# Attention backward on one core: the four dV quarters of a block, one in each even unit and ahead of the output transposes

## The chip, the cores and the metric

The kernel runs on one core of one Trainium2 chip, in one launch. The metric is the device time of that core in microseconds (us); less is better. PE is TensorE (matmuls and transposes), ACT is ScalarE, DVE is VectorE, POOL is GpSimd, SP is the engine whose queue issues most DMAs.

## What is computed

The reference takes two attention layers over the same kind of input (2048 tokens, width 448, 16 heads of 28) and returns their joined output together with the gradients of all eight inputs. Layer A is a linear attention; layer B is a softmax attention in which all 16 heads share one key and one value head. The change is in the backward pass of layer B:

```python
scores = jnp.einsum("bhqd,bkd->bhqk", q, k) * (Dh ** -0.5)
p = _softmax(scores, axis=-1)
o = jnp.einsum("bhqk,bkd->bhqd", p, v)
_out, _vjp = jax.vjp(_f, A_x, A_wqkv, A_wo, B_x, B_wq, B_wk, B_wv, B_wo)
_grads = _vjp(grad_out)
```

For layer B the core loop needs, for every pair of heads and every group of queries, the exponentials E of the scores, the output O = E V / sum, the gradient dP = dO Vᵀ, the product dS = E * dP (the row term is folded into an added column), and from these dQ = dS K, dK = dSᵀ Q and dV = Eᵀ dO.

## The kernel before, in words

Layer A and the projections of layer B come first (the span's first 208 us). Then the core loop `for u in range(NU + 28)` (from L926) runs over 512 **units** and a tail. A **block** b is 8 units: two heads and 256 queries against all 2048 keys; a unit takes two tiles of 128 keys. There are 64 blocks. In this document "unit k" means any u with u % 8 = k. All instructions are issued in the order in which the code is written (`manual_schedule`), so each engine's queue has that order, and only semaphores make it wait.

The loop is a software pipeline, and one pass of it works on several blocks at once. In unit u:

- `rows_SD` (L683) puts eight **row matmuls** on PE (tiles of 32 rows by 128 columns, 256 elements each): four give the scores of unit u in two PSUM banks (`aacc`, two of the three in `SB`), four give dP of unit u - 16 in the two banks `DB` (`agen`). In odd units the order is score 0, score 1, dP 0, dP 1, and again; in even units the two matmuls of dP 1 come last.
- ACT takes three instructions: the exponential of score 0 (L946, "exp 0"), the copy of dP 1 to `cp` (L960), the exponential of score 1 (L992, "exp 1"). DVE multiplies dP 0 by E to the first half of `dsT` (L958), POOL does the second half out of `cp` (L961), and DVE transposes the `dsT` of unit u - 18 in 32 x 32 squares to `dsx` (L1039).
- In odd units `dk_m` puts 16 dK matmuls on PE (tiles of 32 x 32, 512 elements). In even units `o_dq` puts 16 matmuls for O and dQ of two units on PE (tiles of 128 rows by 32 columns, 256 elements).

Some work comes once in a block, through the third bank of `SB`, called `spare`. It is the bank that exp 1 of unit u - 1 reads and that score 0 of unit u + 1 is written to:

- unit 2: `onat_T` (L806) puts the block's end product O back into its natural layout with two fp32 transposes (PE, L809; tiles of 64 x 128). `o_norm` takes it from there: a reciprocal (DVE, L818) and a product (DVE, L819), both read from `spare`. POOL then makes `prod` and `don` (L823 to L827).
- unit 4: `row_D` (L831, L832) finishes `don`.
- unit 6: `don_T` (L834 to L840) transposes `don` into `spare` (128 x 32 tiles), `don_copy` (DVE, L847) takes it out.
- unit 0 of most blocks: a part of the output projection (`out_proj`, 128 x 32 tiles, 112 columns, or 224 in ten blocks) or, in early blocks, of dO's projection goes through `spare`, and DVE copies it out (L747 or L913).
- unit 1: DVE copies O from the accumulator (L974). Unit 3: DVE copies dQ (L977).

The **dV quarters** are `dv_mm(dv_acc, b, h, qb)` (L896): four matmuls side by side (128 x 32 tiles, 512 elements each) that add head h and query half qb of block b to a PSUM bank of their own. Their moving operand is `eN`, which a DMA transpose on SP's queue makes of four units of exponentials at a time (L994); `eN` has six buffers, two to a block. Their weights are `don`, which has three buffers. Before the change the quarters stand at the end of the PE work of a unit, behind `o_dq`: quarters 0 and 1 of block b in unit 8b + 20 (unit 4), quarter 2 in 8b + 22 (unit 6), quarter 3 in 8b + 26 (unit 2). Unit 0 has none.

Of the kernel before, what the change touches and what calls it, by code (L numbers as in the profile page):

```python
# [25 lines left out]
def kernel(  # L26
# [620 lines left out]
    NB = 64  # L647
# [3 lines left out]
    with ExitStack() as cs_:  # L651
# [20 lines left out]
        def eN(b, c):  # L672
            return ENs[(2 * b + c // 2) % 6][:, 16 * (c % 2):16 * (c % 2) + 16, :]

        def mmt(out, lhsT, rhs, pos, start, stop):
            nc.tensor.matmul(out, lhsT=lhsT, rhs=rhs, start=start, stop=stop, tile_position=pos,  # L676
                             skip_group_check=True)

        def blk(b):
            qc, pair = divmod(b, 8)  # L680
            return qc, pair, pair // 2, pair % 2

        def rows_SD(u, sp, dp):  # L683
            b, tp = divmod(u, 8)
            w = u - 16
            qc, pair, g, hp = blk(b)
            todo = [(0, 0), (0, 1), (1, 0), (1, 1)] * 2
            if sp is not None and dp is not None and u % 2 == 0:
                todo = [(0, 0), (0, 1), (1, 0)] * 2 + [(1, 1)] * 2
            seen = {}  # L690
            for d in todo:
                if (dp if d[0] else sp) is None:
                    continue
                k, h = d
                t2 = seen.get(d, 0)
                seen[d] = 1
                t = 2 * tp + t2
                tc_ = slice(t * P, (t + 1) * P)
                oc = slice(t2 * 256, (t2 + 1) * 256)
                r = 64 * (1 - hp if k else hp) + 32 * h  # L700
                if k:
                    mmt(dp[h][:, oc], vT_rep[r:r + 32, tc_], doT[w // 8][r:r + 32, :], (r, 0), True, True)
                else:
                    mmt(sp[h][:, oc], kT_rep[r:r + 32, tc_], qT_B[g][r:r + 32, qc * 256:(qc + 1) * 256],
                        (r, 0), True, True)
# [96 lines left out]
        def due(u, lag):  # L802
            b, r = divmod(u - lag, 8)
            return b if r == 0 and 0 <= b < NB else None

        def onat_T(b, bank):  # L806
            onp = bank[:, 0:P].rearrange("p (q h c) -> p q h c", q=2, h=2)
            for qb in range(2):
                nc.tensor.transpose(onp[:, qb, :, :].rearrange("p h c -> p (h c)"), oTs[0:64, qb * P:(qb + 1) * P],  # L809
                                    identF[0:64, 0:64], tile_position=(0, 0))  # L810
            onps[b] = onp
# [48 lines left out]
        def dk_m(b, m, other=0):  # L860
            qc, pair, g, hp = blk(b)
            h, B, s = m // 8, (m // 2) % 4, m % 2
            for a in range(4):
                rhs = dsx[b][32 * a:32 * a + 32, :, h, :, :].rearrange(
                    "p u t (b i s) -> p u t b i s", b=4, s=2)[:, :, :, B, :, s]
                k = 32 * ((a + 2) % 4) if other else 32 * a
                mmt((dk_two if other else dk_acc)[k:k + 32, :],
                    qX[qc][32 * a:32 * a + 32, B, s, pair * 64 + 32 * h:pair * 64 + 32 * h + 32],
                    rhs, (32 * a, k), other == 2 or b == 0 and m == 0, other == 0 and b == NB - 1 and m == 15)
# [19 lines left out]
        def o_dq(vs, ys):  # L889
            for v, y in zip(vs, ys):  # L890
                todo = [f(i) for f, i in ((o_mm, v), (dq_mm, y)) if 0 <= i < NU]
                for _ in range(2):
                    for g_ in todo:
                        next(g_)

        def dv_mm(dv_acc, b, h, qb):  # L896
            for c in range(4):
                rhs = eN(b, c).rearrange("p (u h t q) k -> p u h t q k", u=2, h=2,
                                                       t=2)[:, :, h, :, qb, :]
                mmt(dv_acc[32 * c:32 * c + 32, :], don[b][:, qb, h, :], rhs, (0, 32 * c),  # L900
                    b == 0 and h + qb == 0, b == NB - 1 and h + qb == 2)
# [15 lines left out]
        with tc.manual_schedule():  # L917
# [8 lines left out]
            for u in range(NU + 28):  # L926
# [4 lines left out]
                dp = DB if hasD else None  # L931
                spare = SB[(2 * u + 2) % 3] if hasS else DB[u // 4 % 2] if u > 530 else SB[2]
                rows_SD(u, sp, dp)
                if (b := due(u, 10)) is not None:
                    onat_T(b, spare)
                if (b := due(u, 14)) is not None:
# [10 lines left out]
                if u == 1:  # L947
                    q_shift(pn3, shifts[3], [pd_.tile([P, 2, 512], BF16, name="dsT").rearrange("p a b -> p (a b)").bitcast(F32)
                                             for _ in range(1)])
                    dv_acc = psA.tile([P, 512], F32, name="aacc")  # L950
# [48 lines left out]
                if u % 2:  # L999
                    b, i = divmod(u - 27, 8)  # L1000
                    if 0 <= b < NB:
                        for m in range(2 * i, 2 * i + 4):
                            dk_m(b, m, (1 + (u == 519 and m == 2 * i + 1)) * (m % 2) if 519 <= u < 537 else 0)
                else:
                    o_dq((u - 2, u - 1), (u - 20, u - 19))
                    b, n = divmod(u - 20, 8)
                    for k in {0: (0, 1), 2: (2,), 6: (3,)}.get(n, ()) if 0 <= b < NB else ():
                        dv_mm(dv_acc, b, k // 2, k % 2)
                y = u - 18

                if 512 <= u < 528 and u % 2 == 0:
# [23 lines left out]
                if 0 <= y < NU:  # L1035
                    b, tp = divmod(y, 8)
# [115 lines left out]
```

## Time and profile before

| what | value |
|---|---|
| median of 3 runs | 1052.08 us (1051.96 to 1053.91) |
| the profiled execution, its own time | 1052.68 us |
| its span in the trace | 1050.9 us (1.8 us lie outside it) |
| busy in the span: PE, DVE, ACT, POOL | 96%, 85%, 83%, 76% |
| core loop with scores (units 0 to 511) | 207.7 to 977.0 us |
| one block of 8 units, steady | 11.97 and 12.03 us, in turn |
| granted TensorE clock | 1.00 |

A block is found in the trace by ACT's exponentials, of which the loop has 512 pairs, one per unit. Two things help to read the tables. The matmuls' starts are recorded and their ends are modelled, and matmuls on different tiles run side by side, so PE's 96% is the time in which any matmul is open, not time at peak. And where DVE or ACT work back to back, an instruction starts some hundredths of a us before the one ahead of it has ended, so the step from start to start, and not the duration, says what an instruction costs there.

### The profile page before, as it was taken

To read this page: it belongs to the slowest core of one execution; us is meant where nothing else is said; L and a number is where in the kernel's file an instruction comes from. 1 tells how busy PE (TensorE), PEld (TensorE's weight loads), DVE (VectorE), ACT (ScalarE), POOL (GpSimd) and SP (SyncE) were. 2 spreads that over 40 slices of the span, in tenths; PEclk is the share of its full clock that TensorE was granted. 3 is DMA by queue.
4 is the path that set the end of the run, shared out by engine and by line. 5 is a ranking of instruction groups with operands and counts; after the bars stand their busy time and mean duration, and the time that the engine had idled before them with its cause. 6 is when DMAs were issued, how large, how long until landed. Compare 5 with 4: busy or idle time off the path is not lost.

```text
span 1050.9 us, 40033 instructions
## 1 busy us (share of the span) xinstructions
PE 1008.4 (96%) x16236; PEld 486.6 (46%) x16245; DVE 895.9 (85%) x1781; ACT 871.5 (83%) x1743; POOL 798.2 (76%) x1044
## 2 busy tenths in 40 slices
PE   9999999998999999999999999999999999999998
PEld 5555554434444444444444444444444444444444
DVE  6897500669999999999999999999999999999942
ACT  6463122589999999999999999999999999999632
POOL 8601272238888998899899989988998999888860
PEclk9999999999999999999999999999999999999999
DMA  9879999299999999999999999999999999999973
GB/s 266 150 134 192 189 222 215 42 163 202 188 196 190 188 195 198 194 193 191 197 175 195 192 202 185 204 199 184 192 194 191 194 190 193 204 186 182 220 156 87
DMA packets 689058, 195.15 MB, mean 186 GB/s; under 512 B 670408, under 2 KB 686688, under 8 KB 688872
## 3 DMA queue, kind: packets, MB, share of 16 engines
q1 hardware_dynamic: 680392, 179.97, 102.1%
q0 software_dynamic: 4544, 9.46, 3.4%
q10 hardware_dynamic: 3936, 3.16, 1.0%
q8 instruction: 127, 2.08, 0.8%
q14 instruction: 59, 0.48, 0.1%
HBM read 12.60 MB, written 10.84 MB: 22 GB/s over the span
## 4 chain that ended last, share of the span: by engine, by line
PE 44%; ACT 33%; issue 14%; DVE 6%; POOL 2%; DMA 0%; ACTq 0%; DVEq 0%; POOLq 0%
ACT cp L960 17%; ACT eT L992 13%; PE agen L81 13%; PE aacc L676 10%; PE agen L676 10%; PE aacc L81 6%; ACT eT L946 2%; DVE dsT L958 2%; PE aacc L809 2%; DVE dsx L1039 2%; PE aacc L840 1%; POOL dsT L961 1%; DMA out_dram<-dsT 0%; PE agen L313 0%; PE agen L227 0%
## 5 line engine op out<-in xcount | busy, mean ns | idle before, releaser
L961 POOL TENSOR_TENSOR dsT<-cp,eT 128x512 bf16<-128x512 bf16 x512 | 587.7, 1156 | 78.9 <-ACT cp L960 73.2
L1039 DVE STREAM_TRANSPOSE dsx<-dsT 128x512 f32<-128x512 f32 x512 | 357.8, 699 | 2.8 <-POOL dsT L961 0.7
L676 PEld LDWEIGHTS <-R 32*128 32x128 bf16 (+1 forms) x9104 | 228.5, 94 | 275.0 <-issue 239.4
L958 DVE TENSOR_TENSOR dsT<-agen,eT 128x512 bf16<-128x512 f32 x512 | 341.9, 668 | 10.6 <-PE agen L676 5.4
L960 ACT ACTIVATE cp<-agen 128x512 bf16<-128x512 f32 x512 | 315.8, 617 | 11.5 <-PE agen L676 10.5
L946 ACT ACTIVATE eT<-aacc 128x512 bf16<-128x512 f32 x512 | 313.6, 612 | 13.6 <-PE aacc L676 4.3
L992 ACT ACTIVATE eT<-aacc 128x512 bf16<-128x512 f32 x512 | 322.2, 629 | 0.0
L676 PE MATMUL agen<-dsx,qX 32*32 32x512 bf16 x4024 | 264.0, 376 | 0.0
L676 PE MATMUL agen<-doT,R 32*128 32x256 bf16 x2048 | 246.7, 269 | 4.2 <-DVE dsT L958 2.5
L676 PE MATMUL aacc<-R,R 32*128 32x256 bf16 (+1 forms) x2240 | 218.5, 269 | 7.1 <-DVE oTs L819 2.0
L676 PE MATMUL agen<-eT,R 128*32 128x256 bf16 x2048 | 157.4, 274 | 0.1
L676 PE MATMUL agen<-dsT,R 128*32 128x256 bf16 x2048 | 156.6, 274 | 0.1
L676 PEld LDWEIGHTS <-qX 32*32 32x32 bf16 x4096 | 78.2, 89 | 111.7 <-issue 53.3
L676 PE MATMUL aacc<-eN,don 128*32 128x512 bf16 x1024 | 96.7, 379 | 0.0
L81 PEld LDWEIGHTS <-R 128*128 128x128 bf16 x517 | 40.9, 98 | 42.2 <-issue 12.0
L81 PE MATMUL agen<-R,R 128*128 128x448 bf16 (+1 forms) x174 | 41.1, 360 | 1.8 <-ACT R L229 0.8
L851 POOL COPY qst<-R 128x512 bf16<-128x512 bf16 x56 | 34.2, 611 | 2.9 <-DMA qX<-qst 2.8
L823 POOL TENSOR_TENSOR prod<-R,oTs 128x128 f32<-128x128 bf16 x64 | 27.6, 431 | 9.3 <-DVE oTs L819 9.3
L676 PEld LDWEIGHTS <-don 128*32 128x32 bf16 x1024 | 33.8, 97 | 0.5
L586 DVE TENSOR_TENSOR osb<-R 32x512 bf16<-32x512 bf16 x4 | 1.7, 413 | 34.7 <-ACT R L583 34.7
L262 POOL TENSOR_SCALAR wdq<-wdq 128x448 bf16<-128x448 bf16 x16 | 21.1, 1327 | 12.9 <-DVE phiT L243 12.9
L427 POOL COPY pk<-R 128x256 bf16<-128x256 bf16 x4 | 1.6, 399 | 37.7 <-DVE R L389 37.7
(234 smaller groups left out, 983.1 us busy)
## 6 DMA issues: line engine op xcount, KB each, us to landing
eN<-eT SPq DMA_TRANSPOSE x128
xa<-in_A_x_dram SPq DMA_DIRECT2D x8, 224.0 KB
ga<-in_grad_out_dram SPq DMA_DIRECT2D x4, 448.0 KB
out_dram<-osb ACTq DMA_DIRECT2D x16, 112.0 KB
xa<-in_grad_out_dram POOLq DMA_DIRECT2D x4, 448.0 KB, 9.4
out_dram<-wdq POOLq DMA_DIRECT2D x8, 224.0 KB, 5.8
eT<-in_grad_out_dram SPq DMA_DIRECT2D x4, 448.0 KB
eT<-in_B_x_dram SPq DMA_DIRECT2D x4, 448.0 KB
```

The source lines that it names most:

```text
L81: nc.tensor.matmul(out_ap, lhsT=lhsT, rhs=rhs, start=start, stop=stop, tile_position=(0, 0))
L262: nc.gpsimd.tensor_scalar(out=wq_n[:, st, 0:D], in0=wq_n[:, st, 0:D], scalar1=1.0, scalar2=None, op0=ALU.min)
L676: nc.tensor.matmul(out, lhsT=lhsT, rhs=rhs, start=start, stop=stop, tile_position=pos, skip_group_check=True)
L809: nc.tensor.transpose(onp[:, qb, :, :].rearrange("p h c -> p (h c)"), oTs[0:64, qb * P:(qb + 1) * P], identF[0:64, 0:64], tile_position=(0 ...
L823: nc.gpsimd.tensor_tensor(out=prod[b][:], in0=dnv, in1=os_, op=ALU.mult)
L851: eng.tensor_copy(out=st.rearrange("p (b s) a j -> p b s a j", s=2)[:, :, s, :, :], in_=src.unsqueeze(2).to_broadcast([P, 4, 4, 32]))
L946: nc.scalar.activation(out=eT(u)[:, 0, :], in_=sp[0][:, :], func=ACT.Exp, scale=scale)
L958: nc.vector.tensor_tensor(out=dst[:, 0, :], in0=dp[0][:, :], in1=ew[:, 0, :], op=ALU.mult)
L960: nc.scalar.activation(out=cp[:, :], in_=dp[1][:, :], func=ACT.Copy)
L961: nc.gpsimd.tensor_tensor(out=dst[:, 1, :], in0=cp[:, :], in1=ew[:, 1, :], op=ALU.mult)
L992: nc.scalar.activation(out=eT(u)[:, 1, :], in_=sp[1][:, :], func=ACT.Exp, scale=scale)
L1039: nc.vector.transpose(out=dsx[b][:, tp, :, :, :].rearrange("p h t c -> p (h t c)").bitcast(F32), in_=dsT[y][:, :, :].rearrange("p h c -> p ...
```

## The change

The dV quarters move. Each even unit gets one, from 18 to 24 units behind its block's first scores: quarter 0 in unit 8b + 18 (unit 2), 1 in 8b + 20 (unit 4), 2 in 8b + 22 (unit 6), 3 in 8b + 24 (unit 0). They are issued right behind `rows_SD`, ahead of `onat_T`, `don_T` and the projections' part, and no longer behind `o_dq`. The order of the quarters among themselves, and with it the accumulation, stays. No instruction is added or taken away.

```diff
                 rows_SD(u, sp, dp)
+                if u % 2 == 0:
+                    b, n = divmod(u - 18, 8)
+                    if 0 <= b < NB:
+                        dv_mm(dv_acc, b, n // 4, n // 2 % 2)
                 if (b := due(u, 10)) is not None:
                     onat_T(b, spare)
                 if (b := due(u, 14)) is not None:
                     don_T(b, spare)
...
                 else:
                     o_dq((u - 2, u - 1), (u - 20, u - 19))
-                    b, n = divmod(u - 20, 8)
-                    for k in {0: (0, 1), 2: (2,), 6: (3,)}.get(n, ()) if 0 <= b < NB else ():
-                        dv_mm(dv_acc, b, k // 2, k % 2)
```

The orders of PE's work in the four even units, before and after:

| unit | before | after |
|---|---|---|
| 0 | rows, projection, O and dQ | rows, dV 3, projection, O and dQ |
| 2 | rows, O transposes, O and dQ, dV 3 | rows, dV 0, O transposes, O and dQ |
| 4 | rows, O and dQ, dV 0, dV 1 | rows, dV 1, O and dQ |
| 6 | rows, `don` transposes, O and dQ, dV 2 | rows, dV 2, `don` transposes, O and dQ |

## The prediction

> **What bounds the kernel now.** First the page: busy times and the chain.
>
> ```profile
> PE 1008.4 (96%) x16236; PEld 486.6 (46%) x16245; DVE 895.9 (85%) x1781; ACT 871.5 (83%) x1743; POOL 798.2 (76%) x1044
> ...
> PE 44%; ACT 33%; issue 14%; DVE 6%; POOL 2%; DMA 0%; ACTq 0%; DVEq 0%; POOLq 0%
> ```
>
> PE looks like the bound, and moving PE work into a hole of PE looks like a gain. So I read the timeline of one block, and in it the place where most of the change happens: unit 2, with the first instructions of unit 3 (columns: start, duration, engine, line, what).
>
> ```profile
> 521.18 0.60 ACT L960 ACTIVATE cp<-agen 128x512 bf16<-128x512 f32 x1
> ...
> 521.77 0.44 PE L676 MATMUL agen<-doT,R 32*128 32x256 bf16 x3
> ...
> 522.32 0.20 PEld L809 LDWEIGHTS aacc<-identF,oTs 64*128 64x128 f32 x2 [0.40 <-ACT eT L992]
> 522.33 0.33 PE L809 MATMUL aacc<-identF,oTs 64*128 64x64 f32 x2
> 522.59 0.34 PEld L676 LDWEIGHTS <-R 128*32 128x32 bf16 x16
> ...
> 522.87 0.16 DVE L818 RECIPROCAL rl<-aacc 128x4 f32<-128x4 f32 x1
> ...
> 523.04 0.39 PE L676 MATMUL aacc<-eN,don 128*32 128x512 bf16 x4
> 523.06 0.29 DVE L819 TENSOR_TENSOR oTs<-aacc,rl 128x128 f32<-128x128 f32 x1
> ...
> 523.40 0.28 PE L676 MATMUL aacc<-R,R 32*128 32x256 bf16 x2
> ...
> 523.82 0.60 ACT L946 ACTIVATE eT<-aacc 128x512 bf16<-128x512 f32 x1
> ```
>
> There is a hole in front of the O transposes: they wait for exp 1 of unit 1 to leave `spare`. The dV quarter at 523.04 lies between the O and dQ matmuls and the rows of unit 3, and exp 0 of unit 3 starts at 523.82, 0.74 after exp 1 of unit 2 (523.08), where ACT's step is 0.48 when nothing holds it. So 0.26 is lost here. Over units 1, 3, 5, 7 of the steady blocks the loss is 0.05, 0.25, 0.05 or 0.17 (in turn), 0.10 or 0.05; 24 steps of 0.477 are 11.45, a block takes 11.97 or 12.03.
>
> Who releases the rows of unit 3? The product L819 reads `spare`, and score 0 of unit 3 goes to that bank. It ends at 523.06 + 0.29 = 523.35, the rows start 0.05 later, and that 0.05 holds in all 47 blocks between 303 and 870 us (0.052 to 0.054). Unit 18 of the loop has no dV quarter yet, and there the wait is seen openly:
>
> ```profile
> 231.40 0.29 DVE L819 TENSOR_TENSOR oTs<-aacc,rl 128x128 f32<-128x128 f32 x1
> ...
> 231.75 0.28 PE L676 MATMUL aacc<-R,R 32*128 32x256 bf16 x2 [0.30 <-DVE oTs L819]
> ```
>
> PE sat idle for 0.30 where the quarter would have been, and the rows came no earlier. The rows of units 1 and 7 likewise start 0.05 after DVE's copy out of `spare` (L747, L847). And DVE has no room here: from its product of unit 1 (L958) to that of unit 4 every step from start to start is the same in every block and next to the smallest found, 4.93 or 5.05 us in all, by the parity of the block. The dP rows of unit 5 wait for that last product, and behind them exp 0 of unit 5 (the loss of 0.17 or 0.05). So the block is a ring: ACT from unit 5 to unit 1, DVE from unit 1 to unit 5. PE lies in it only with the transposes that release DVE.
>
> **The change part by part.** *Quarters taken from the ends of units 2, 4, 6:* each spares PE some 0.2 (two quarters last 0.60, one 0.39), at places where the rows wait for DVE anyway. I take 0. In unit 5 the first rows may start earlier, but the dP rows wait for L958 of unit 4. Bounds: 0, and a gain of what PE alone would lose (rival C).
>
> *The quarter ahead of the O transposes, unit 2.* Two rows for a change of tile shape, from unit 4:
>
> ```profile
> 512.88 0.49 PE L676 MATMUL agen<-doT,R 32*128 32x256 bf16 x3
> 513.29 0.28 PE L676 MATMUL agen<-eT,R 128*32 128x256 bf16 x2
> ...
> 513.74 0.60 PE L676 MATMUL aacc<-eN,don 128*32 128x512 bf16 x8
> 514.28 0.28 PE L676 MATMUL aacc<-R,R 32*128 32x256 bf16 x2
> ```
>
> From rows to 128 x 32 the next start is 0.08 before the modelled end (513.37); from dV to another shape 0.06 before it (514.34). In unit 2 the rows end at 521.77 + 0.44 = 522.21, so dV starts at 522.13 and ends at 522.52, and the transposes start at 522.46, not 522.33: 0.13 late. The hole, 0.20 wide, does not hold a quarter and its change of shape. They end at 522.79 (0.33 long). How long DVE then needs shows where it was idle and waiting, in block 0:
>
> ```profile
> 219.54 0.33 PE L809 MATMUL aacc<-identF,oTs 64*128 64x64 f32 x2
> ...
> 219.98 0.18 DVE L818 RECIPROCAL rl<-aacc 128x4 f32<-128x4 f32 x1
> ```
>
> 0.11 after their end. So the reciprocal can start at 522.90; it started at 522.87, 0.21 after the end. Of the 0.13, 0.10 is cover and 0.03 is paid. Behind the waiting reciprocal stand L819, and behind that the rows of unit 3 and the rest of DVE's run up to unit 5: the whole ring shifts. 62 such units: 62 x 0.03 = **+1.9**. The trace shows no change from 128 x 32 to 64 x 128, so both ends: without a drain the transposes follow after a quarter's step (0.22, from the eight matmuls of unit 4), at 522.35, within the cover: 0. If they wait for the quarter's end and a semaphore's 0.05, at 522.57, the reciprocal starts 0.14 late: 62 x 0.14 = +8.7. I take 0.03, by the dV row of unit 4, the same departure to a shape of other height.
>
> The Trainium skill (TensorEngine Tiling (Array Packing), Key Properties) says that changing the tiling mode, not just the tile, drains TensorE. That speaks against this change, since unit 2 goes from three changes of shape to four; the rows above agree (about 0.1 over the matmul's own step at each), and by this rule the 0 end falls away.
>
> *The quarter ahead of the projection, unit 0.* Same shape, so no drain: dV at 519.20, the projection 0.22 later at 519.42 instead of 519.38: 0.035 late. DVE's copy starts 0.12 after its end, with DVE idle just ahead of it, so it shifts by 0.035; so do the rows of unit 1. With 112 or 128 columns the second score row waits 0.05 longer for `cp` anyway, and DVE's transpose has 0.03 of room: I take 0.01 for 46 blocks, **+0.5** (0 to 1.6). With 224 columns (ten blocks, where unit 1 loses 0.29) nothing covers: 10 x 0.035 = **+0.35**.
>
> *The quarter ahead of the `don` transposes, unit 6:* 0.04 late, same shape, while their copy starts 0.21 after their end: hidden, 0; without that cover it would be 62 x 0.04 = 2.5. *Unit 4:* O and dQ 0.22 later, still done before the rows: 0.
>
> *DMAs and data:* nothing is added. Quarters 0 and 3 come two units (3 us) earlier, but the DMA transposes of `eN` are issued with exp 1 of units 3 and 7 and last 5.5 us each, so the second ends some seven units ahead of unit 18; `don` is done in unit 13. SP's transposes wait for ACT, never for dV; its buffers come free earlier and nobody waited. No queue but PE's changes. The tail has the same quarters, up to two units earlier: 0, within 1 us.
>
> **The sum:** 1.9 + 0.5 + 0.35 = +2.75 us. The profiled execution took 1052.68 (span 1050.9 and 1.8 outside it), so 1055.4; it lies 0.6 above the median, so **1054.8** against 1052.08. About 0.2% (2.1 us) is what a measurement of this kernel can tell from no change.
>
> **The rivals.**
>
> A, *cover holds*: the drain or DVE's 0.11 is some hundredths shorter, the reciprocal does not wait, and unit 0 alone pays: +0.85 at most, 1052.5 to 1053. For it: 0.10 of 0.13 is covered, and the rest is as small as the error of a modelled end. Against: both rows are of this kind. Chance 0.30.
>
> B, *full drain*: the fp32 transposes wait for the quarter's end, and start 0.19 to 0.24 late: 62 x 0.10 to 0.14 + 0.85 = +7 to +9.5, 1059 to 1061.5. [...] Against: in block 0 transposes follow rows as fast as anything else does. Chance 0.15.
>
> C, *the chain is right* and PE sets the start of units 3 and 7; faster. The page's chain runs through PE here (L676 44% with PE's other lines). Then the quarter's 0.20 less the transposes' 0.13 gives 0.07 in unit 3 of 62 blocks (4.3), and 0.05 in unit 7 of every other one (1.6): -5.9 + 0.85, 1047. It decides if the rows of unit 3 start before L819 has ended. Against: the 0.05 behind L819 in every block, and unit 18. Chance 0.12.
>
> D, the change does nothing of what it says: not possible in a written order. The forecast itself: 0.43.
>
> **How the numbers follow.** Forecast 1053.9 to 1056.8. A and B stretch the range to 1050.5 (a microsecond of disturbance and the tail below A) and 1059.5 (B's lower part); C and B's upper part, under 0.2, stay outside. Faster by over 0.2%: C, 0.12, and 0.02 of A: 0.14. Slower: B, 0.15, and 0.38 of the forecast: 0.53. Within: the rest of A and of the forecast, 0.33.
>
> **What would show it.** Right: dV in front of L809 in unit 2, L809 about 0.13 later after the last dP row, the wait in front of it gone, and the reciprocal 0.11 after its end instead of 0.21; the rows of unit 3 still 0.05 behind L819; blocks of 12.00 and 12.06. In unit 0, ten wide blocks 0.03 longer. Wrong: the rows of unit 3 follow PE and not L819, or DVE's run from unit 1 to 5 gets shorter; then blocks fall under 11.95.

## The result and the profile after

The changed kernel takes 1055.19 us (median of 19 runs, 1053.99 to 1056.39), the kernel before, run beside it, 1053.49 (19 runs). The ratio is 1.0019, with a 95% interval of 1.0012 to 1.0027: 1.3 to 2.8 us slower, with 2.0 in the middle (the two medians lie 1.7 us apart). The forecast was 2.75 us slower.

First the page of the changed kernel, its lines of busy times and of the chain:

```profile
PE 1009.8 (96%) x16236; PEld 484.2 (46%) x16245; DVE 898.8 (85%) x1781; ACT 871.1 (83%) x1743; POOL 799.6 (76%) x1044
...
DVE 45%; PE 31%; issue 10%; POOL 8%; ACT 5%; DVEq 0%; DMA 0%; POOLq 0%; ACTq 0%
```

The busy times stand as before to 3 us. The chain has gone over from PE and ACT (44% and 33%) to DVE and PE (45% and 31%), though the same instructions run and the time moved by 0.2%. Here engines that release each other within hundredths of a us trade places in the chain for almost nothing. What changed is seen in unit 2 (timeline of the changed kernel; columns: start, duration, engine, line, what; line numbers past 932 are 4 higher than before, and behind `dv_mm`'s old place 1 higher):

```profile
545.43 0.62 ACT L996 ACTIVATE eT<-aacc 128x512 bf16<-128x512 f32 x1
...
545.54 0.44 PE L676 MATMUL agen<-doT,R 32*128 32x256 bf16 x3
...
545.91 0.40 PE L676 MATMUL aacc<-eN,don 128*32 128x512 bf16 x4
...
546.24 0.20 PEld L809 LDWEIGHTS aacc<-identF,oTs 64*128 64x128 f32 x2 [0.23 <-ACT eT L996]
546.24 0.33 PE L809 MATMUL aacc<-identF,oTs 64*128 64x64 f32 x2
...
546.68 0.18 DVE L818 RECIPROCAL rl<-aacc 128x4 f32<-128x4 f32 x1
...
546.90 0.29 DVE L819 TENSOR_TENSOR oTs<-aacc,rl 128x128 f32<-128x128 f32 x1
...
547.25 0.28 PE L676 MATMUL aacc<-R,R 32*128 32x256 bf16 x2
...
547.66 0.60 ACT L950 ACTIVATE eT<-aacc 128x512 bf16<-128x512 f32 x1
```

Read it from above. The quarter fills the hole behind the dP rows, and the transposes start 0.33 behind it. In the kernel before, they waited for exp 1 of unit 1 to leave `spare`. In the block that the prediction shows, this is its line:

```profile
521.65 0.62 ACT L992 ACTIVATE eT<-aacc 128x512 bf16<-128x512 f32 x1
```

It ended at 522.27 and the transposes started 0.06 later, at 522.33. In the changed kernel exp 1 ends at 546.05 and the transposes start 0.19 later. The profile still puts the 0.23 for which the weight load sits idle down to exp 1, the last semaphore that it sees, but by these times the transposes now wait behind the quarter. They end at 546.57, and the reciprocal starts 0.11 later: it waits for them now. The rows of unit 3 come 0.06 behind the end of L819 (547.19; 0.053 in the median, as before), and exp 0 of unit 3 behind them. In numbers, as medians over the steady blocks (us, each from the row ahead of it):

| place | before | after | predicted |
|---|---|---|---|
| unit 2: last dP row to transposes, starts | 0.384 | 0.525 | 0.51 |
| end of transposes to reciprocal | 0.207 | 0.106 | 0.11 |
| last dP row to reciprocal, starts | 0.926 | 0.966 | + 0.03 |
| reciprocal to rows of unit 3, starts | 0.537 | 0.561 | the same |
| end of L819 to rows of unit 3 | 0.053 | 0.053 | the same |
| loss in unit 3 | 0.25 | 0.31 to 0.32 | 0.28 |
| steady blocks, in turn | 11.97, 12.03 | 12.03, 12.09 | 12.00, 12.06 |
| unit 0: last dP row to projection, starts | 0.382 | 0.421 | + 0.035 |
| loss in unit 1, wide projections | 0.29 | 0.32 | + 0.035 |
| loss in unit 1, narrow projections | 0.05 to 0.06 | 0.05 to 0.08 | + 0.01 |
| unit 6: end of `don` transposes to their copy, in turn | 0.20, 0.29 | 0.18, 0.25 | still covered |

From exp 0 of unit 0 to that of unit 511 the core loop takes 771.9 us where it took 769.35: +2.56. Block by block, 60 of the 64 give +3.75 in sum, and four others -1.19 (block 5: -0.82, 7: -0.17, 29: -0.39, 32: +0.19). The span grew by less than the loop, by 1.55: the stretch ahead of the first exponential is 0.58 shorter in this trace, the one behind the last 0.44. The next section asks for these parts.

### The profile page after: what moved, and what is told of

Its sections match the earlier page's. It is cut to its first block, busy times and chain, and to the rows that moved or that the text cites. A ratio compares the mean times of both kernels' runs of the same rounds, so it can differ in the third digit from the quotient of the medians.

```text
span 1052.5 us, 40040 instructions
## 1 busy us (share of the span) xinstructions
PE 1009.8 (96%) x16236; PEld 484.2 (46%) x16245; DVE 898.8 (85%) x1781; ACT 871.1 (83%) x1743; POOL 799.6 (76%) x1044
## 4 chain that ended last, share of the span: by engine, by line
DVE 45%; PE 31%; issue 10%; POOL 8%; ACT 5%; DVEq 0%; DMA 0%; POOLq 0%; ACTq 0%
DVE dsx L1040 18%; DVE dsT L962 17%; PE agen L81 13%; POOL dsT L965 7%; PE agen L676 6%; PE aacc L81 6%; PE aacc L676 5%; ACT cp L964 3%; DVE oTs L978 2%; DVE R L981 2%; DVE oTs L819 2%; DVE doT L847 1%; ACT eT L996 1%; DVE rl L818 1%; DVE Dq L831 1%
## 5 line engine op out<-in xcount | busy, mean ns | idle before, releaser
L676 PEld LDWEIGHTS <-R 32*128 32x128 bf16 (+1 forms) x9104 | 243.9, 94 | 253.1 <-issue 201.2
L676 PE MATMUL aacc<-R,R 32*128 32x256 bf16 (+1 forms) x2240 | 221.3, 269 | 19.0 <-DVE doT L847 6.1
L676 PE MATMUL aacc<-eN,don 128*32 128x512 bf16 x1024 | 102.4, 390 | 0.0
L676 PEld LDWEIGHTS <-don 128*32 128x32 bf16 x1024 | 26.3, 93 | 53.8 <-issue 53.8
L262 POOL TENSOR_SCALAR wdq<-wdq 128x448 bf16<-128x448 bf16 x16 | 21.1, 1326 | 12.2 <-DVE phiT L243 12.2
```

Source lines behind the costliest of these rows:

```text
L262: nc.gpsimd.tensor_scalar(out=wq_n[:, st, 0:D], in0=wq_n[:, st, 0:D], scalar1=1.0, scalar2=None, op0=ALU.min)
```

## The experiments

**Theory:** the whole cost is the quarter ahead of the O transposes in unit 2, which makes DVE's reciprocal wait. **Rivals:** the cost comes from the quarters' new places elsewhere (unit 0, 4, 6); the added change of tile shape costs by itself; or PE, which the page shows 96% busy, holds units 3 and 7 after all (rival C).

### Unit 2's quarter alone, taken out of the change and put in alone

Out of the change (`e1_q0_behind`; the other three units as changed):

```diff
+                if u % 8 == 2:
+                    if (b := due(u, 10)) is not None:
+                        onat_T(b, spare)
                 if u % 2 == 0:
                     b, n = divmod(u - 18, 8)
                     if 0 <= b < NB:
                         dv_mm(dv_acc, b, n // 4, n // 2 % 2)
-                if (b := due(u, 10)) is not None:
-                    onat_T(b, spare)
```

> The changed kernel, but in unit 2 the dV quarter stands behind the O transposes and ahead of O and dQ; units 0, 4 and 6 stay as changed. Theory (the O transposes in unit 2 release DVE's run, and only their delay costs): the transposes start 0.38 us after the last dP row again as before the change, unit 3 loses 0.25 instead of 0.31, blocks are 11.97 and 12.03 again, and only the ten wide parts of the projection keep 0.03 each: +0.3 us on the kernel before, 3.5 us under the changed one. Rival (the cost lies in units 0, 4, 6, or in four quarters spread over four units): unit 3 keeps 0.31 and the time stays at the changed kernel's.

Alone (`e2_q3_ahead`; the kernel before with one quarter ahead of the transposes):

```diff
                 rows_SD(u, sp, dp)
+                if (b := due(u, 26)) is not None:
+                    dv_mm(dv_acc, b, 1, 1)
...
-                    for k in {0: (0, 1), 2: (2,), 6: (3,)}.get(n, ()) if 0 <= b < NB else ():
+                    for k in {0: (0, 1), 2: (2,)}.get(n, ()) if 0 <= b < NB else ():
```

> The kernel before, with one part of the change alone: its quarter of unit 2 (quarter 3) is put ahead of the O transposes, and the others stay behind O and dQ in units 4 and 6. Theory: the whole cost is there. The transposes start 0.525 after the last dP row, the reciprocal 0.04 later than before, unit 3 loses 0.31, blocks are 12.03 and 12.09: +0.06 in 62 blocks, +4 us in the sum of the blocks. Rival (the cost comes from the other units): as before, 11.97 and 12.03.

Measured: with the quarter behind the transposes, 1053.49 against 1053.53, ratio 1.0000 (0.9991 to 1.0008). Transposes at 0.384, reciprocal 0.208 behind their end, unit 3 loses 0.25, blocks 11.97 and 12.03; only the wide projections keep their +0.03 in unit 1. With it alone ahead of them, 1056.13, ratio 1.0020 (1.0010 to 1.0030): 0.525, 0.107, 0.32, blocks 12.04 and 12.09. One edit in one unit makes the whole difference, in both directions. The moves in units 0, 4 and 6 together cost nothing that the time of a whole run can tell; the forecast had +0.85 for them, which such a time could not have told either.

### The same change of shape, under the cover

If the drain by itself cost something, half a quarter ahead of the transposes should show it. `e5_half_ahead` splits unit 2's quarter into two halves of 256 elements, one ahead of the transposes and one behind them. (`dv_mm` gets the halves as its last two arguments; its own lines are left out of the cut. A part of dV is lost by the split, so this kernel serves for its time alone.)

```diff
...
-                        dv_mm(dv_acc, b, n // 4, n // 2 % 2)
+                        dv_mm(dv_acc, b, n // 4, n // 2 % 2, 0, 1 if n == 0 else 2)
                 if (b := due(u, 10)) is not None:
                     onat_T(b, spare)
+                if (b := due(u, 18)) is not None:
+                    dv_mm(dv_acc, b, 0, 0, 1, 2)
```

> The changed kernel, with the quarter of unit 2 in two halves (256 of the 512 elements each): one half ahead of the O transposes, one behind them, so four matmuls more. The number of changes of tile shape in unit 2 is that of the changed kernel, four. Theory (the cost is the delay beyond a cover of 0.10): the transposes start 0.42 after the last dP row, 0.03 late, all under cover; unit 3 loses 0.25, blocks 11.97 and 12.03, +0.3 us on before. Rival (a change of shape ahead of the transposes costs by itself, however short the quarter): unit 3 keeps at least 0.03 of the 0.06.

```profile
546.60 0.29 PE L676 MATMUL aacc<-eN,don 128*32 128x256 bf16 x4
546.82 0.20 PEld L809 LDWEIGHTS aacc<-identF,oTs 64*128 64x128 f32 x2
546.82 0.34 PE L809 MATMUL aacc<-identF,oTs 64*128 64x64 f32 x2
...
547.09 0.29 PE L676 MATMUL aacc<-eN,don 128*32 128x256 bf16 x4
547.33 0.16 DVE L818 RECIPROCAL rl<-aacc 128x4 f32<-128x4 f32 x1
```

The timeline of unit 2 in that kernel: transposes 0.22 behind the half quarter, reciprocal 0.17 behind their end (547.16), at its old place after the rows. Time 1053.98, ratio 1.0006 (0.9997 to 1.0014), unit 3 loses 0.25, blocks 11.97 and 12.03. The change of shape is there and costs nothing as long as it lies within DVE's cover. Beside the step of 0.33 with a whole quarter it also prices the change: to a matmul of its own shape half a quarter takes a step of 0.12 (547.09 to the O matmuls at 547.21 in this kernel) and a whole one 0.22 (below), so 0.10 and 0.11 are left. The Trainium skill (TensorEngine Tiling (Array Packing), Key Properties) says that changing the tiling mode drains TensorE. The trace agrees as far as a step of that size goes, which does not grow with the matmul ahead of it. Whether all of it is a drain is not shown: the load of the fp32 weights starts together with the transposes in both kernels and could have a part in it.

### Double the dose

`e9_two_ahead`: the changed kernel with quarters 0 and 1 both ahead of the transposes, none in unit 4.

```diff
-                    if 0 <= b < NB:
-                        dv_mm(dv_acc, b, n // 4, n // 2 % 2)
+                    for k in {0: (0, 1), 4: (2,), 6: (3,)}.get(n, ()) if 0 <= b < NB else ():
+                        dv_mm(dv_acc, b, k // 2, k % 2)
```

> The changed kernel, with two quarters (0 and 1) ahead of the O transposes in unit 2 and none in unit 4; 2 and 3 stay. Theory (beyond the cover of 0.10, delay is paid one for one): the transposes start 0.525 + 0.217 = 0.74 after the last dP row, so unit 3 loses 0.217 more than in the changed kernel, 0.53 instead of 0.31: 62 x 0.22 = +13.5 us on the changed kernel, +15.5 on before. Rival (part of a delay is always taken up by unit 5, which waits for DVE or cp, whichever is later): unit 5 loses less, and at most 0.12 in every other block comes back, +10 us on the changed kernel.

```profile
551.14 0.61 PE L676 MATMUL aacc<-eN,don 128*32 128x512 bf16 x8
...
551.69 0.33 PE L809 MATMUL aacc<-identF,oTs 64*128 64x64 f32 x2
...
552.13 0.18 DVE L818 RECIPROCAL rl<-aacc 128x4 f32<-128x4 f32 x1 [0.19 <-PE aacc L809]
```

Its timeline: the transposes start 0.55 behind the quarters, 0.22 more than with one, and the profile now names the wait of the reciprocal for them. Time 1067.61, ratio 1.0143 (1.0127 to 1.0160): +15.1. Unit 3 loses 0.52 to 0.53, blocks are 12.25 and 12.31. With the cover used up, what PE has more ahead of the transposes is paid in full: 0.21 to 0.22 in unit 3 of each steady block.

### Does freeing PE in unit 2 bring anything? (rival C)

`e3_no_q_in_2`: the kernel before with unit 2's quarter moved to the end of unit 0.

```diff
-                    for k in {0: (0, 1), 2: (2,), 6: (3,)}.get(n, ()) if 0 <= b < NB else ():
+                    for k in {0: (0, 1), 2: (2,), 4: (3,)}.get(n, ()) if 0 <= b < NB else ():
```

> The kernel before, with quarter 3 moved from the end of unit 2 to the end of unit 0 (two units earlier), both times behind O and dQ: PE has 0.2 us less to do between the O transposes and the rows of unit 3. Theory (those rows wait for DVE's product): unit 3 loses 0.25 as before, the rows start 0.05 after the product; in unit 0 the copy of the projection's part releases the rows of unit 1 some 0.2 earlier than PE's end, so a quarter (0.2 more) at that end can make unit 1 lose up to 0.15 more: 0 to +9 us. Rival (PE's chain sets unit 3): unit 3 loses 0.07 instead of 0.25, -0.18 in every block, -11 us less what unit 1 gives back.

```profile
549.87 0.16 DVE L818 RECIPROCAL rl<-aacc 128x4 f32<-128x4 f32 x1
550.06 0.29 DVE L819 TENSOR_TENSOR oTs<-aacc,rl 128x128 f32<-128x128 f32 x1
...
550.40 0.28 PE L676 MATMUL aacc<-R,R 32*128 32x256 bf16 x2 [0.20 <-DVE oTs L819]
```

The end of unit 2 in that kernel: PE stands idle for 0.20 where the quarter was, and the rows still come 0.05 behind L819. Unit 3 loses 0.25 as before. Rival C falls: in the kernel before, DVE and not PE sets unit 3. Where the quarter went, PE did become late: in most blocks unit 1 loses 0.14 to 0.18 instead of 0.05 to 0.06, because its rows now start 0.19 after the copy out of `spare`, behind the quarter. Ratio 1.0024 (1.0014 to 1.0034). So rows that start 0.05 behind DVE do not tell how much room PE has ahead of them: the end of unit 2 holds a quarter, and at the end of unit 0 it costs some 0.1 us a block.

### Shorter DVE work ahead of the reciprocal

If DVE's run from unit 1 to unit 5 sets the block, the copies in it (L974 for O, L977 for dQ) are worth their length, and in the changed kernel, where the reciprocal waits for PE, the O copy is worth nothing. Two kernels cut one of the copies from 256 to 64 columns in the kernel before (0.41 to 0.21, 0.43 to 0.23), one cuts the O copy in the changed kernel. (One fence shows both edits. The two kernels with a short O copy also fill all of `oTs` with 1.0 once, in u = 7, where the others fill half of it with 0.)

```diff
-                    nc.vector.tensor_copy(out=oTs[0:64, :], in_=oq[0:64, 0:256])
+                    nc.vector.tensor_copy(out=oTs[0:64, 0:64], in_=oq[0:64, 0:64])
...
-                    nc.vector.tensor_scalar(out=qT_B[g][64 * hp:64 * hp + 64, qc * 256:(qc + 1) * 256],
-                                            in0=oq[64:128, 0:256], scalar1=scale, scalar2=None, op0=ALU.mult)
+                    nc.vector.tensor_scalar(out=qT_B[g][64 * hp:64 * hp + 64, qc * 256:qc * 256 + 64],
+                                            in0=oq[64:128, 0:64], scalar1=scale, scalar2=None, op0=ALU.mult)
...
```

dQ's copy, kernel before: 

> The kernel before, with DVE's copy of dQ in unit 3 cut to 64 of its 256 columns (three quarters of dQ are left out). DVE's run from unit 1 to unit 4 is some 0.2 us shorter behind the product L819. Theory (the run sets exp 0 of unit 5): unit 3 keeps 0.25; unit 5 loses 0.05 in all blocks instead of 0.17 and 0.05 in turn, so every other block is 0.12 shorter: -3.6 us, and no more, since behind DVE the copy to cp holds unit 5 at 0.05. Rival (PE is the bound): no block changes, within 0.5 us.

O's copy, kernel before: 

> The kernel before, with DVE's copy of O in unit 1 cut to 64 of its 256 columns (three quarters of O are left out). DVE's run is some 0.2 us shorter ahead of the reciprocal, whose cover over the O transposes is 0.10. Theory: the reciprocal comes 0.10 earlier and then waits for the transposes (0.106 after their end, as in the changed kernel), which costs it 0.024 of overlap: unit 3 loses 0.17 to 0.18 instead of 0.25, every block is 0.076 shorter: -4.7 us. Rival (PE is the bound): within 0.5 us. Rival (DVE's total is the bound): 62 x 0.2 = -12 us.

O's copy, changed kernel: 

> The changed kernel, with the same cut of O's copy in unit 1. Theory: there the reciprocal waits for PE's transposes already, so a shorter copy ahead of it brings nothing to it: unit 3 keeps 0.31, unit 5 its losses, the time stays at the changed kernel's within 0.5 us, and some 6.5 us above the kernel before with the same cut. Rival (DVE sets unit 3 in the changed kernel as well): it gains as much as the kernel before does.

Measured:

| cut | time | ratio to before | unit 3 | unit 5 | blocks |
|---|---|---|---|---|---|
| dQ copy, before | 1051.44 | 0.9983 (0.9974 to 0.9992) | 0.25 | 0.05 in all | 11.93 |
| O copy, before | 1051.98 | 0.9991 (0.9982 to 0.9999) | 0.22 | as before | 11.94, 11.99 |
| O copy, changed | 1054.90 | 1.0018 (1.0009 to 1.0027) | 0.31 to 0.32 | as changed | 12.03, 12.09 |

The dQ copy behaved as expected in the blocks, and the time gave half of it. For the O copy the expectation of the kernel before was half missed, and its timeline of unit 2 says why:

```profile
546.26 0.18 DVE L818 RECIPROCAL rl<-aacc 128x4 f32<-128x4 f32 x1
546.48 0.29 DVE L819 TENSOR_TENSOR oTs<-aacc,rl 128x128 f32<-128x128 f32 x1
546.53 0.39 PE L676 MATMUL aacc<-eN,don 128*32 128x512 bf16 x4
...
546.85 0.28 PE L676 MATMUL aacc<-R,R 32*128 32x256 bf16 x2
```

The reciprocal starts 0.10 earlier and 0.11 behind the transposes, and L819 now ends at 546.77. But the rows start 0.08 behind that end and no longer 0.05, so they do not wait for DVE any more: they come 0.32 behind the quarter started at 546.53, the step from a quarter to rows that unit 4 shows too (the quarters' last 0.22 behind 513.74, the rows at 514.28). So PE was only 0.03 to 0.05 short of being the one that sets this place: of the 0.08 by which L819 ends earlier, the rows gained 0.05. In the changed kernel the same cut brings nothing (ratio 1.0018 beside its own 1.0019, the same blocks): there the reciprocal waits for PE. One number of that expectation was missed: the two kernels with a short O copy were to lie 6.5 us apart. By their steady blocks they do, to within half a us (0.10 in a block), but the times lie 2.9 apart.

### A version meant to gain, and what it ran into

In every other block unit 5 loses 0.17 because DVE's run is late. `e8_dq_copy_later` moves the dQ copy of the kernel before out of that run, from unit 3 to unit 4. So that the next block's dQ can begin meanwhile, odd blocks gather dQ in the other half of the bank (the last block as it is).

```diff
-                    mmt(oq[64 + 32 * h:96 + 32 * h, 0:256], kn[:, t, :],
+                    mmt(oq[64 + 32 * h:96 + 32 * h, 256 * (b % 2):256 * (b % 2) + 256], kn[:, t, :],
...
-                if (b := due(u, 27)) is not None:
+                b = NB - 1 if u == 8 * NB + 19 else due(u, 28)
+                if b is not None and (b < NB - 1 or u == 8 * NB + 19):
...
```

> The kernel before, with DVE's copy of dQ moved out of its run: dQ of odd blocks goes to the other half of the accumulator's bank, so that the copy can be made in unit 4, behind the product, instead of unit 3, ahead of its transpose (the last block's stays). dV is where it was. Theory (from unit 1 to unit 4 DVE's run sets when exp 0 of unit 5 starts): the run is about 0.5 us shorter, unit 5 loses 0.05 in all blocks instead of 0.05 and 0.17 in turn, so every other block is 0.12 shorter: about -3.7 us; unit 3 keeps 0.25, since the copy stands behind the product L819. Rival (PE's work, 96% busy, is the bound, as the page has it): DVE's run doesn't matter, the time stays within 0.5 us.

```profile
602.74 0.69 DVE L958 TENSOR_TENSOR dsT<-agen,eT 128x512 bf16<-128x512 f32 x1
602.82 0.62 ACT L946 ACTIVATE eT<-aacc 128x512 bf16<-128x512 f32 x1
...
603.65 0.43 DVE L978 TENSOR_SCALAR R<-agen 64x256 bf16<-64x256 f32 x1
...
604.13 0.29 PE L676 MATMUL agen<-eT,R 128*32 128x256 bf16 x2 [1.25 <-DVE R L978]
...
605.54 0.60 ACT L946 ACTIVATE eT<-aacc 128x512 bf16<-128x512 f32 x1 [1.12 <-PE agen L676]
```

A clear miss: 1123.41, ratio 1.0677. The timeline of unit 4 shows both halves of it. DVE's run did get shorter: L958 of unit 4 starts 0.08 ahead of exp 0 of its unit, where it stood 0.40 to 0.52 behind. But the first O matmul of unit 4, which in this block writes neither the rows nor the columns that the copy reads, waits 1.25 for the copy, and the rows of unit 5 stand behind it on PE. The wait is in the program: the other half of one bank was not free of it. Whether a bank of its own would have brought the gain was not tried.

### Where two microseconds went: the odd blocks

In five of these kernels (the change, `e2_q3_ahead`, `e3_no_q_in_2`, `e9_two_ahead`, `e10_dq_copy_short`) the time moved 1.7 to 2.2 us less than the steady blocks add up to, and in `e11_o_copy_short` 1.0 less. So both kernels were traced a second time, without a change.

Before: 

> The kernel before, unchanged, for a second trace: which of its losses come back. The regular ones (units 1, 3, 5, 7) must. If the irregular ones (1.2 us in blocks 5 and 7, 0.4 in block 29, 0.2 to 0.3 in blocks 15, 32, 39, 49) sit elsewhere or have other sizes, a difference of a microsecond between two single traces says nothing, and the regular losses alone tell what the change did.

After: 

> The changed kernel, unchanged, for a second trace. Unit 3 loses 0.31 to 0.32 in every regular block again; blocks 12.03 and 12.09. Irregular losses as in the kernel before, in place and size by chance; if instead they are smaller in both traces of the changed kernel, they are what hides part of the 4 us that the regular blocks lose.

The steady losses came back to a hundredth (unit 3: 0.25, and 0.31 to 0.32). The irregular ones moved: in the kernel before, block 5 took 12.49 instead of 13.24, block 7 12.44 instead of 12.19, block 29 gave its 0.45 back and blocks 38 (12.63) and 55 (12.26) lost. In the changed kernel block 29 took 12.54 instead of 12.03 and block 7 12.15 instead of 12.03, while block 5 stayed (12.43 and 12.47). So two of the terms of the -1.19 above are one trace's own, and a difference of two profiled executions is good to about 1 us here.

Put side by side, the two pairs of traces (before and after, us) also show that the odd blocks are not all of it:

| where | first pair | second pair |
|---|---|---|
| sixty blocks | +3.75 | +4.01 |
| the four blocks that moved most | -1.19 | -0.49 |
| ahead of the first exponential | -0.58 | -0.63 |
| behind the last exponential | -0.44 | -0.57 |
| the whole span | +1.55 | +2.33 |

In both pairs about 1 us is lost from sight outside the core loop. Ahead of it nothing was changed, and its length goes from 207.1 to 207.9 over all the kernels without an order that follows their edits, so that part looks like chance. The tail does follow them: it takes 73.45 to 73.66 us in the kernels whose quarter 3 comes two units earlier and 73.69 to 74.08 in the others (75.5 in `e8_dq_copy_later`). That the earlier quarters shorten it is likely, and no run takes them out of the tail alone.

Blocks 5 and 7 lie where POOL waits for a DMA (waits of POOL in the kernel before, from 255 to 310 us; columns: us in total, times, longest):

```profile
POOL qst L851 <- DMA qX<-qst: 2.8, 2, 1.9
```

POOL may not write the staging buffer of the queries before the `qX` transpose of the last one has gone through SP's queue, where two `eN` transposes of 5.2 to 5.5 us stand in each block, and in blocks 4 to 7 one of `qX` of 1.3 besides (11.9 to 12.2 together in this trace). `e14_qst_two_later` issues copies and transpose two units later.

```diff
-                gq, iq = divmod(u % 64 - 30, 8)
+                gq, iq = divmod(u % 64 - 32, 8)
```

> The kernel before, with the two copies of queries on POOL (L851) and the DMA transpose of qX behind the second one issued two units later (in units 0 and 1 of a block instead of 6 and 7 of the one ahead; four blocks of every eight up to unit 448); nothing else is moved. What it asks: the measured times moved by about 2 us less than the steady blocks added or saved, in both directions, and the difference stood in blocks that lose more than the steady ones, 5 and 7 above all (13.24 and 12.19 in one trace of the kernel before, 12.49 and 12.44 in another; together 1.0 to 1.5 over steady). Theory: SP's queue. In blocks 4 to 7 it holds two transposes of eN of 5.2 to 5.5 us and one of qX of 1.3 in a block, 12.0 to 12.3 against a block of 11.97; the copy on POOL waits 1.2 to 1.9 for the qX transpose ahead of it, and then POOL has late what the don transposes of unit 6 wait for. Two units (3 us) later that transpose is done: POOL's wait for qX goes from 2.8 to 0, blocks 5 and 7 fall to 11.97 to 12.10, steady blocks stay: 1.0 to 1.4 us faster than the kernel before. Rival: POOL is late for its own work, the copies (0.61 each, on an engine with 0.3 of room in a unit), and the wait only shows it: then they delay unit 4's don from units 0 and 1 as well: the wait goes, blocks 5 and 7 stay over 12.2, blocks 4 and 6 may join them: no change, or up to 1 us slower.

Measured: 1054.02, ratio 1.0006 (0.9997 to 1.0015): no gain. The wait is gone from POOL's list, and blocks 5 and 7 take 12.01 both: their loss came from SP's queue, as the theory had it. But five other blocks (21, 29, 37, 45, 53) now take 12.58 to 12.62, where they took 11.97 (29: 12.42), most of it in unit 7. The waits of block 21, from 457 to 470 us:

```profile
PE aacc L840 <- POOL don L832: 0.8, 1, 0.8
```

There the two copies, with the issue of an output store (L749, 0.62) between them, make `prod` and `don` late on POOL for the `don` transposes of unit 6. It is the rival's mechanism, in other blocks than it named. Both hold. By the traces blocks 5 and 7 gain 0.9 to 1.4 and the five others lose 2.7 to 3.1, so the move is rather a loss, of a size that the times can't tell from nothing. What stays open is whether such losses shrink when all blocks get longer. That SP's queue, with some 12 us of transposes in such a block, lags less behind blocks of 12.03 and 12.09 would fit blocks 5 and 7 of the changed kernel. But `e3_no_q_in_2` speaks against it: its blocks are longer still (12.09 and 12.14 there), and yet POOL waits 3.7 us for `qX` in the same stretch, and blocks 5 and 7 take 13.27 and 12.72.

## Why the prediction was right, and where it was off

- **What bounds the kernel:** right. The rows of unit 3 stay 0.053 behind L819 in both kernels, and freeing PE there brings nothing (`e3_no_q_in_2`). The page's chain, 44% PE before and 45% DVE after, told neither.
- **Quarters taken from the ends of units 2, 4, 6, at 0:** right; the changed kernel with unit 2's quarter behind the transposes takes the time of the kernel before. One reading was too wide: the rows of unit 7 start 0.05 behind the copy out of `spare` only in every other block, and 0.12 behind it in the rest. There PE was late, and the change takes that away (0.05 in all blocks), but the loss in unit 7 stays, 0.05 and 0.10 in turn.
- **The quarter ahead of the O transposes:** the mechanism was right to the row: 0.14 late (0.13 predicted), 0.10 of it covered, the rest paid, the rows still behind L819. The size was off: **62 x 0.03 = +1.9** came to +3.8 in unit 3 in both pairs of traces (with the irregular blocks put at the steady ones): 0.064 in most blocks, 0.05 in the early ones and in those with wide projections, nothing in the first two. Of the 0.064, 0.040 is the reciprocal's later start (0.141 less 0.101; the 0.03 was rounded down on the way), and 0.024 was not in the sum at all: a reciprocal that begins after a wait takes 0.18 and hands on after 0.217, where the overlapped one took 0.157 and handed on after 0.192. The block 0 row that the prediction showed for its 0.11 had the 0.18 in it, beside the 0.16 of unit 2.
- **Unit 0:** right for the wide projections, +0.03 in ten blocks. The narrow ones cost 0.01 in twelve early blocks and nothing in the others, so the term of +0.85 came to +0.45 to +0.5. **Unit 6:** right, hidden. **The tail:** 0.4 to 0.6 shorter, within the microsecond that was allowed for it.
- **Rival A** (cover holds) falls: the reciprocal waits for the transposes in every steady block, and only with half a quarter does the cover hold. **Rival B** (full drain) falls: 0.14 late, not 0.19 to 0.24. **Rival C** falls by `e3_no_q_in_2`; it was near, though: with DVE earlier, PE is next late after some 0.05 (`e11_o_copy_short`).
- **The time:** +2.0 measured (1.3 to 2.8), +2.75 predicted. Part of that nearness is luck. The term of unit 2 was too small by 1.9, so that the steady blocks came to about +4, and the odd blocks and the stretches outside the loop, which the sum left out or put at 0, took some 2 us of it back. That the odd blocks are other work (DMA transposes on SP's queue and POOL's copies) is shown for blocks 5 and 7. Why they and the stretches outside the loop cost the changed kernel less stays open.

## What to carry to other kernels

Ask for every hole of a busy engine whose wait it stands in: a hole ahead of an instruction that releases the bounding engine is cover of a known width, and the work put there is free up to that width (a half quarter: 0) and costs its full step beyond it (two quarters: 15 us). When an instruction turns from overlapped to waiting, price its own longer step too, and not the later start alone. Read gains and losses of a few hundredths from the steady blocks of a trace, and the time of the whole from many runs: the two differed by 2 us here, in a few irregular blocks and outside the loop.

## What the runs showed of the hardware

- A DVE reciprocal of 128x4 that starts after a wait costs 0.024 to 0.026 us more than one that starts in the shadow of the operation ahead of it: step to the next start 0.217 against 0.192.
- The change from the 128 x 32 quarter to the 64 x 128 transposes costs 0.10 to 0.11 over the step of the matmuls ahead of it, with 256 as with 512 elements a matmul (0.22 against 0.12, and 0.33 against 0.22, from start to start).
- A matmul into rows and columns of a PSUM bank that a DVE copy does not read still waited 1.25 for that copy, by the semaphores of the program.
